# Loads of V issued on ScalarE's queue, loads of K on SyncE's

## The chip, the core and the metric

The kernel runs on one core of one Trainium2 chip. The core has five engines with instruction streams of their own (TensorE, VectorE, ScalarE, GpSimd, SyncE) and 16 DMA engines that move data from HBM to the on-chip memory SBUF. The metric is the device time of one execution in microseconds. Three executions of the kernel before took 669.8, 670.45 and 670.9 us; the median, 670.45 us, is the time that the change is measured against.

## The reference

One step of decoding with a cache, beside a gated MLP that shares its input. For 4 batch entries, 32 heads, 4096 cached positions and heads of 128 elements, all in bfloat16:

```python
xn = layernorm(x)                                   # x: (4, 1, 640)
q = (xn @ wq).reshape(B, Sq, H, Dh)                 # one query per head and batch entry
scores = einsum('bhqd,bhkd->bhqk', q, k_cache) * Dh ** -0.5
p = softmax(scores)
o = einsum('bhqk,bhkd->bhqd', p, v_cache)
out = x + o.reshape(B, Sq, H * Dh) @ wo + gmlp(xn)  # gmlp: w_in, gelu, layernorm, gate, w_out
```

K and V are read once each: 2 x 4 x 32 x 4096 x 128 elements of 2 bytes, 268 MB. The weights add some 14 MB. Each byte of the cache is used for one query alone, so the arithmetic is small beside the reading.

## The kernel before, in words

**Units.** The 32 heads are cut into `NG = 8` groups of `HG = 4`. A unit is one group and one batch entry, so there are `NU = 32` units, numbered u = 4g + b. Of each unit a K tile and a V tile of 4 MiB are loaded (128 partitions of 32 KiB): K0 to K31 and V0 to V31. Each is used in `NCH = 4` chunks.

**Buffers.** All these tiles, and before them three tiles of weights, come from one pool, `kvpool`, with five buffers that are handed out in turn. So the load of a tile waits until the tile five places earlier in the order of loads has been used up. The order alternates: K4, V0, K5, V1, K6, V2 and so on. So V(n) waits until K(n+2) is used up, and K(n) until V(n-7) is.

**What uses a tile.** A chunk of K is transposed by VectorE (`emit_T`, line 318, into `ktpool` with two buffers) and multiplied with the queries on TensorE (`emit_S`, line 336), which adds to the scores S of the group in PSUM. K is used up with its fourth transposition. When the scores of a group are complete, `softmax_max` and `softmax_exp` find the maximum and let ScalarE compute the exponentials (line 364), `softmax_t` transposes them on TensorE (line 377), and `z_fill` lets ScalarE copy them into the two operand buffers `Zb[0]` and `Zb[1]` (line 388; eight copies each). `emit_V` multiplies a chunk of V with them (line 422, eight matmuls); V is used up with its fourth chunk, 32 matmuls. After two units of V, `emit_O` copies the result from PSUM on ScalarE (line 430), and `emit_sel`, `emit_oT`, `emit_proj` bring it into the output projection.

**The order of the work.** One loop over steps s writes it down: K(u) is loaded at step 4u and transposed at 4u to 4u+3; V(v) is loaded at step 18 + 4v (`VD = 18`) and used at 18 + 4v to 21 + 4v; the softmax of group g stands at step 16g + 17. The framework (Tile) takes this as a priority, works out all waits, and may place an instruction ahead of another on its engine's stream where it reckons that it can start sooner.

**Queues.** All loads of K, V and wo stand on SyncE's queue, in the order of the source, each with its waits. ScalarE's queue issues three small loads at the start and half of the output at the end.

**The end.** V31 is treated apart: it is loaded in four pieces (`TAIL`, of 64, 32, 16 and 16 of its 128 rows), is the stationary operand of 128 small matmuls (line 534), and these wait for the pieces one by one. They accumulate in the one PSUM buffer (`ps_o`) that V30's result is copied out of first. After them come the projection (line 460) with `wo_last`, a cast and the output. `wo_last` is loaded in three pieces (line 299).

```python
        elif v == NU - 1 and vc == 0:
            g = NG - 1
            emit_O(g, 1)
            emit_selL(1, 1)
            ...
            ol_ps = ps_o.tile([P, HG], F32, tag="O", name="ol")
```

Of the kernel before, what the change touches and what calls it, by code (L numbers as in the profile page):

```python
# [16 lines left out]
def kernel(  # L17
# [19 lines left out]
    nc = tc.nc  # L37
    P = 128
    B, Sq, D = A_x.shape
    _, H, Sk, Dh = A_k_cache.shape  # L40
# [10 lines left out]
    NU = NG * B  # L51
# [33 lines left out]
    def kv_tile(name):  # L85
        return kvpool.tile([P, KV], BF16, tag="kv", name=name)
# [85 lines left out]
    for bb in range(2):  # L172
        nc.vector.tensor_copy(out=SelG[:, bb, :, :, 2 * bb:2 * bb + 2],
                              in_=I32[:].rearrange("p (b h c) -> p c h b", b=2, c=NCH))
# [13 lines left out]
    for hd in range(HG):  # L188
        nc.vector.tensor_copy(out=Pm[:, :, hd, :].rearrange("p (a w) j -> p a w j", w=2),
                              in_=ident_bf[:].rearrange("p (a j w) -> p a w j", a=2, w=2))  # L190
# [47 lines left out]
    t1 = const.tile([P, FC, B], F32)  # L238
# [45 lines left out]
    def load_unit(cache, key, u, cuts=(0, T)):  # L284
        g, b = divmod(u, B)
        t_sb = kv_tile(f"{key}{u}")
        src = cache[b, g * HG:(g + 1) * HG].rearrange("e (m t) d -> (e m) (t d)", t=T)
        for t0, t1 in zip(cuts[:-1], cuts[1:]):
            nc.sync.dma_start(out=t_sb[:, t0 * Dh:t1 * Dh], in_=src[:, t0 * Dh:t1 * Dh])
        state[(key, u)] = t_sb  # L290

    def load_wo(g):
# [197 lines left out]
    for s in range(NS):  # L490
        u, ch = divmod(s, NCH)
        if ch == 0 and u < NU:
            load_unit(A_k_cache, "k", u)
        v, vc = divmod(s - VD, NCH)
        if vc == 0 and 0 <= v < NU:
            load_unit(A_v_cache, "v", v, cuts=TAIL if v == NU - 1 else (0, T))
# [75 lines left out]
```

## Time and profile before

| What | Value |
|---|---|
| Median of three executions | 670.45 us |
| Profiled execution, its own time | 670.88 us |
| Its span, first to last instruction | 669.1 us |
| Moved by DMA in the span | 282.65 MB, 422 GB/s on the mean |
| Busy: TensorE / VectorE / ScalarE | 50% / 48% / 9% of the span |
| Loads of K and V, size and median time from issue to landing | 4 MiB; 43.3 us (K), 41.1 us (V) |
| Mean granted TensorE clock | 0.743 of full speed |

The span leaves out 1.8 us around the first and last instruction. A load's time from issue to landing holds the time that it waits behind earlier loads. In the profile, PE is TensorE, DVE is VectorE, ACT is ScalarE, SP is SyncE; a q behind the name (ACTq, SPq) is the engine's sequencer, which issues DMAs and handles waits.

### The profile page before, as it was taken

How to read it: one execution, taken by the hardware profiler on the slowest of the kernel's cores; microseconds unless marked ns; L12 is line 12 of the kernel's file. 1: busy time of each engine (PE TensorE's matmuls, PEld its weight loads, DVE VectorE, ACT ScalarE, POOL GpSimd, SP SyncE). 2: the span in 40 equal slices, each digit the busy share in tenths (PEclk: the TensorE clock that was granted, in tenths of full speed). 3: DMA queues.
4: the chain of work that ended last, by engine and by line, in shares of the span. 5: the costliest groups of instructions: out<-in, count | busy, mean ns of one | idle time of the engine just before them, and what ended most of it. 6: DMA issues, size and time to landing. Idle time of an engine off the chain costs nothing.

```text
span 669.1 us, 6401 instructions
## 1 busy us (share of the span) xinstructions
PE 335.7 (50%) x2781; PEld 139.1 (21%) x2781; DVE 319.5 (48%) x253; ACT 60.4 (9%) x184; POOL 8.9 (1%) x40
## 2 busy tenths in 40 slices
PE   0647463546543664337555364454753366433745
PEld 0511121122111221113121031111311122111323
DVE  4279853465533455542555534346543355543300
ACT  0200210012000210003000030001200021000300
POOL 0010000000000000000000000000000000000000
PEclk9997777778777787676766677866767878567676
DMA  8999999999999999999999999999999999999995
GB/s 313 439 424 428 436 433 428 425 436 431 426 435 430 428 434 439 424 428 434 427 429 433 432 427 434 426 427 441 428 431 430 431 427 432 433 433 426 435 418 230
DMA packets 12900, 282.65 MB, mean 422 GB/s; under 512 B 1621, under 2 KB 3017, under 8 KB 4169
## 3 DMA queue, kind: packets, MB, share of 16 engines
q1 hardware_dynamic: 12568, 282.25, 98.6%
q8 instruction: 21, 0.34, 0.2%
q10 hardware_dynamic: 304, 0.01, 0.0%
q14 instruction: 7, 0.05, 0.0%
HBM read 282.25 MB, written 0.01 MB: 422 GB/s over the span
## 4 chain that ended last, share of the span: by engine, by line
DMA 56%; PE 15%; issue 13%; DVE 12%; ACT 3%; ACTq 0%; DVEq 0%
DMA k<-in_A_k_cache_dram 50%; DVE kT L318 8%; PE O L422 6%; DMA wo_last<-in_A_wo_dram 5%; PE S L336 3%; ACT p L364 3%; PE misc L439 2%; DMA sb_bf<-in_B_b_sp_dram 2%; PE x L377 1%; DVE m L343 1%; DVE om L442 1%; PE misc L251 1%; PE misc L347 1%; ACT O_sb L430 0%; PE zT_ps L209 0%
## 5 line engine op out<-in xcount | busy, mean ns | idle before, releaser
L318 DVE STREAM_TRANSPOSE kT<-k 128x2048 f32<-128x2048 f32 x128 | 284.6, 2280 | 215.0 <-DMA k<-in_A_k_cache_dram 212.4
L336 PE MATMUL S<-kT,QZ 128*32 128x512 bf16 x1024 | 203.7, 538 | 257.6 <-DVE kT L318 255.2
L336 PEld LDWEIGHTS <-QZ 128*32 128x32 bf16 x1024 | 57.3, 115 | 399.1 <-issue 386.7
L422 PE MATMUL O<-v,Zb 128*32 128x512 bf16 x992 | 93.1, 467 | 9.0 <-DMA v<-in_A_v_cache_dram 9.0
L422 PEld LDWEIGHTS <-Zb 128*32 128x32 bf16 x992 | 42.1, 112 | 41.0 <-issue 26.2
L364 ACT ACTIVATE p<-S,negmax 128x1024 bf16<-128x1024 f32 x16 | 17.7, 1109 | 272.0 <-DVE negmax L358 272.0
L430 ACT COPY O_sb<-O 128x512 f32<-128x512 f32 x16 | 9.4, 585 | 240.6 <-PE O L422 240.6
L388 ACT COPY Zb<-x 32x128 bf16<-32x128 bf16 x128 | 27.3, 255 | 10.2 <-PE x L377 9.5
L377 PE MATMUL x<-IdP,p 128*128 128x128 bf16 x128 | 16.1, 305 | 18.9 <-ACT p L364 18.6
L442 DVE SCALAR_TENSOR_TENSOR om<-misc,rinv,MkH 16x512 bf16<-16x512 f32 x7 | 5.2, 739 | 37.8 <-PE misc L439 37.8
L439 PE MATMUL misc<-O_sb,SelG 128*16 128x128 f32 x112 | 16.9, 289 | 2.0 <-DVE rinv L398 1.5
L377 PEld LDWEIGHTS <-p 128*128 128x128 bf16 x128 | 12.0, 138 | 22.6 <-ACT p L364 22.6
L275 POOL COPY QZ<-q 32x16 bf16<-32x16 bf16 x32 | 7.9, 246 | 455.4 <-PE S L336 420.9
L439 PEld LDWEIGHTS misc<-O_sb,SelG 128*16 128x16 f32 x112 | 10.1, 99 | 7.9 <-ACT O_sb L430 2.4
L474 DVE TENSOR_TENSOR oL<-misc,rinv 128x8 bf16<-128x8 f32 (+1 forms) x2 | 0.3, 168 | 22.6 <-PE misc L472 22.6
L343 DVE TENSOR_REDUCE m<-S 128x1 f32<-128x512 f32 x8 | 5.5, 691 | 10.2 <-PE S L336 10.2
L147 PE MATMUL misc<-ident_bf,wq 4*128 4x4 bf16 x5 | 0.4, 178 | 18.9 <-DVE wq L143 18.9
L368 DVE TENSOR_TENSOR rowsum<-rs 128x1 f32<-128x1 f32 x8 | 1.2, 155 | 17.0 <-ACT p L364 17.0
L347 PE MATMUL misc<-dg,ones_f 128*128 128x128 f32 x16 | 3.9, 324 | 9.0 <-DVE dg L345 9.0
L364 ACT ACT_TABLE_LOAD x1 | 1.3, 1283 | 54.8 <-DVE negmax L358 54.8
L460 PE MATMUL proj<-wo,oT 128*4 128x320 bf16 x56 | 5.0, 298 | 1.9 <-DVE oT L453 1.9
L251 PE MATMUL misc<-xnT,wq 128*128 128x4 bf16 x160 | 4.7, 166 | 1.1 <-issue 0.8
(93 smaller groups left out, 75.9 us busy)
## 6 DMA issues: line engine op xcount, KB each, us to landing
k<-in_A_k_cache_dram SPq DMA_DIRECT2D x32, 4096.0 KB, 43.3
v<-in_A_v_cache_dram SPq DMA_DIRECT2D x31, 4096.0 KB, 41.1
wo<-in_A_wo_dram SPq DMA_DIRECT2D x7, 640.0 KB, 44.6
wq<-in_A_wq_dram SPq DMA_DIRECT2D x1, 3072.0 KB, 19.5
w_gmlp<-in_B_w_in_dram SPq DMA_DIRECT2D x1, 2160.0 KB, 9.3
wq<-in_A_wq_dram SPq DMA_DIRECT2D x1, 2048.0 KB
v<-in_A_v_cache_dram SPq DMA_DIRECT2D x1, 2048.0 KB
v<-in_A_v_cache_dram SPq DMA_DIRECT2D x1, 1024.0 KB, 38.4
```

The lines of the kernel that those rows point to most:

```text
L251: nc.tensor.matmul(q_ps[:, h, :], lhsT=wq_t[c][:, h * Dh:(h + 1) * Dh], rhs=xnT[:, c, :], start=(c == 0), stop=(c == DC - 1))
L318: nc.vector.transpose(kT[:], kw[:, ch * n:(ch + 1) * n])
L336: nc.tensor.matmul(S_ps[32 * q:32 * q + 32, :, :], lhsT=qz[:, b, kw, w0:w0 + 32], rhs=kT[:, i, :, kw // 2, :, kw % 2], start=(b == 0 and c ...
L343: nc.vector.tensor_reduce(out=m1[:], in_=S_ps[:].rearrange("p k m -> p (k m)"), axis=AX.X, op=ALU.max)
L347: nc.tensor.matmul(mm[:], lhsT=ones_f[:], rhs=dg[:], start=True, stop=True)
L364: nc.scalar.activation(out=p_i[:], in_=S_ps[:, 8 * i:8 * i + 8, None, :].to_broadcast((P, 8, HG, M)), func=ACT.Exp, bias=negmax[:, 0:1], s ...
L377: nc.tensor.transpose(x[:, t, :], p_bf[t // 8][:, t % 8].rearrange("p h m -> p (h m)"), IdP[:])
L388: nc.scalar.copy(out=dst, in_=src[:, 2 * bb + b1])
L422: nc.tensor.matmul(O_ps[32 * q:32 * q + 32, :, :], lhsT=Zb[bb][:, w0:w0 + 32], rhs=vv[:, e // 16, e % 16, :, :], start=(b1 == 0 and e < 4) ...
L430: nc.scalar.copy(out=O_sb[:], in_=O_ps[:])
L439: nc.tensor.matmul(oh[:], lhsT=SelG[:, bb, c].rearrange("p h b -> p (h b)"), rhs=O_sb[:, c, :], start=(bb == 0 and c == 0), stop=(bb == 1 ...
L442: nc.vector.scalar_tensor_tensor(out=om[:], in0=oh[:, None, :].to_broadcast((G, HG, Dh)), scalar=state.pop(("rinv", g))[:, 0:1], in1=MkH[: ...
```

## The change

The loads of V0 to V30 are issued by ScalarE, those of K and of V31, and of wo, still by SyncE. Sizes, buffers, waits for buffers and all other work are as they were.

```diff
     def load_unit(cache, key, u, cuts=(0, T)):
         g, b = divmod(u, B)
         t_sb = kv_tile(f"{key}{u}")
+
+        eng = nc.scalar if key == "v" and u < NU - 1 else nc.sync
         src = cache[b, g * HG:(g + 1) * HG].rearrange("e (m t) d -> (e m) (t d)", t=T)
         for t0, t1 in zip(cuts[:-1], cuts[1:]):
-            nc.sync.dma_start(out=t_sb[:, t0 * Dh:t1 * Dh], in_=src[:, t0 * Dh:t1 * Dh])
+            eng.dma_start(out=t_sb[:, t0 * Dh:t1 * Dh], in_=src[:, t0 * Dh:t1 * Dh])
         state[(key, u)] = t_sb
```

## The prediction

> **What bounds the kernel now.** I read the page's slices and queues first, then the waits of SyncE's queue, then the timeline of the last 30 us. The DMA row of the page (busy share of the DMA engines in 40 slices, and GB/s) and its list of queues:
>
> ```profile
> DMA  8999999999999999999999999999999999999995
> GB/s 313 439 424 428 436 433 428 425 436 431 426 435 430 428 434 439 424 428 434 427 429 433 432 427 434 426 427 441 428 431 430 431 427 432 433 433 426 435 418 230
> q1 hardware_dynamic: 12568, 282.25, 98.6%
> ```
>
> Only the first and the last slice are not full. Stretch by stretch the answer is the same; the last two columns are DMA share and GB/s:
>
> ```profile
> 500.00:600.00 100.00, 45.63 (x370) 18.21 (x368) 46.95 (x30) 7.38 (x23) 0.00 (x0) 0.75 1.00 430
> 660.00:665.00 5.00, 3.13 (x101) 2.80 (x99) 0.17 (x1) 0.00 (x0) 0.00 (x0) 0.52 0.42 154
> ```
>
> So the transfers bound the time, and one queue keeps them busy. SyncE's waits show why it does: loads wait for buffers (DVE: K used up; PE: V used up), long before their data are needed.
>
> ```profile
> SPq L289 <- DVE kT L318: 303.3, 32, 14.4
> SPq L289 <- DMA k<-in_A_k_cache_dram: 131.2, 30, 7.6
> SPq L289 <- PE O L422: 110.9, 27, 10.3
> ```
>
> At the end (TensorE's timeline from 644 us) the data come in the order of the queue, and TensorE waits for each:
>
> ```profile
> 644.46 3.60 PE L422 MATMUL O<-v,Zb 128*32 128x512 bf16 x32 [5.54 <-DMA v<-in_A_v_cache_dram]
> ...
> 654.18 3.19 PE L422 MATMUL O<-v,Zb 128*32 128x512 bf16 x32 [3.51 <-DMA v<-in_A_v_cache_dram]
> ...
> 658.06 1.06 PE L472 MATMUL misc<-I,O_sb 128*128 128x8 f32 x8 [0.47 <-ACT O_sb L430]
> 659.11 1.79 PE L534 MATMUL ol<-Zb,v 128*128 128x4 bf16 x64
> 661.58 1.02 PE L534 MATMUL ol<-Zb,v 128*128 128x4 bf16 x32 [0.68 <-DMA v<-in_A_v_cache_dram]
> ...
> 664.10 0.59 PE L534 MATMUL ol<-Zb,v 128*128 128x4 bf16 x16 [0.70 <-DMA v<-in_A_v_cache_dram]
> 664.95 1.28 PE L460 MATMUL proj<-wo_last,oL 128*4 128x320 bf16 x8 [0.26 <-DMA wo_last<-in_A_wo_dram]
> ```
>
> V29 lands at 644.4, V30 at 654.15, V31's last piece at 664.05: **9.75 us a load** at full rate. V30's work (654.18 to 659.11) is hidden under V31's transfer. After the last piece lie only 0.6 us of matmuls and the way out: 669.1 - 664.05 = 5.05 us.
>
> **What the Trainium skill says.**
> (1) "DMA: Bandwidth & Descriptors", Issuing engines are not separate DMA queues: transfers issued by different engines run on the same 16 DMA engines and interleave; a second issuer saves only issuing time. The trace agrees as far as it goes: 98.6% of 16 engines' span is already one queue's.
> (2) Same page, Queues, rings and completion order: each DMA engine goes round-robin between the rings that have work. I read that as half the rate for each of two busy rings. No run here shows it: ScalarE's queue is idle through the loop.
> (3) Same page, Where 436 GB/s comes from: the ports' ceiling is 435.2 GB/s. The trace's 430 to 431 is 1% below.
> (4) "Perfetto Trace Analysis", DMA Instruction — HWDGE: the issuing sequencer itself waits for a DMA's semaphores before it goes on. So whatever stands behind a waiting load on ScalarE's stream waits too, and a load behind a waiting instruction of the sequencer is late. The trace has such waits on ScalarE: one before nearly each copy of O, for V's matmuls.
>
> ```profile
> L430 ACTq EVENT_SEMAPHORE  x14: 17/17/17, 155.3 to 648.1; - x14
> ```
>
> **The change part by part.**
>
> *Issue.* 31 issues of 0.33 us (SyncE's timeline: 0.33 for each load of V) leave SyncE and come to ScalarE: 10.2 us over a span in which ScalarE is busy 60.4 us. Cost 0, hidden under the transfers; without that cover at most one issue before each of 8 exponentials, 2.6 us. SyncE gains nothing: it waits for buffers, not for itself.
>
> *Place in ScalarE's stream.* Decisive. Is V(n)'s load placed where the source has it (step 18+4n, when V(n) is needed at once), or where its buffer comes free (K(n+2) used up, step 4n+11)? The trace shows that streams are not in source order. The source has eight copies of Zb, the copy of O, eight copies of Zb; ScalarE's timeline has nine, one, seven:
>
> ```profile
> 230.21 1.97 ACT L388 COPY Zb<-x 32x128 bf16<-32x128 bf16 x9 [1.13 <-PE x L377]
> 234.26 0.58 ACT L430 COPY O_sb<-O 128x512 f32<-128x512 f32 x1 [2.08 <-PE O L422]
> 234.74 1.54 ACT L388 COPY Zb<-x 32x128 bf16<-32x128 bf16 x7
> ```
>
> TensorE too runs four chunks of S and then 32 matmuls of V, where the source alternates. So instructions go where they are reckoned ready, and I take it that V's loads keep about their present times. Then ScalarE's work stands well to them: V(4g+1) waits for K(4g+3), which the exponentials need anyway. At worst the exponentials of group g stand behind V(4g+2), which waits for K(4g+4).
>
> *Middle of the kernel.* With two rings at half rate, K(n+4) and V(n) land together, 19.5 us after the pair before, instead of K first and V 9.75 later. Let a pair land at t. K's four transpositions (8.9 us: 254.72 to 263.61 in VectorE's timeline) free its buffer at t+8.9. V's matmuls free the other by t+12, or, at a group's end, by about t+20 (before: K31's transpositions start at 613.84, V27's matmuls end at 633.3). The pair landing at t+19.5 was issued before t. The pair after needs its loads at t+19.5: V's comes at t+8.9, K's by t+20 at the worst, so one ring at least always has work. In the worst order (exponentials behind V(4g+2)): K(4g+4) is used up at t+28.4, V(4g) at t+28.4+8+3 = t+39.5; K(4g+7) is issued then, and its turn is at t+58.5. The transfers never run dry: cost 0. What two interleaved streams do to the rate itself, no row shows. Bounds: up to the ceiling, 1% or 6.3 us gained over 656 us of transfers; 2%, 13 us, lost, the spread of the page's slices about 430. I take 0.
>
> *End.* K30 and V26 land at 604 (V26's matmuls start at 604.12 now; the bytes moved by then are the same), K31 and V27 at 623.4; K31 now lands at 613.8, so it is a load later. From 623.4 ScalarE's ring holds V28, V29, V30; SyncE's is empty until K31 is used up, 623.4+8.9 = 632.3, when V31's pieces are issued (now 622.75). V28 runs alone, to 633. Then V29 and V31 share: both land near 652.5. **V30 is last**, alone, whole. Group 7's exponentials (now 12.4 us, Zb 17.6 us after K31's landing, so about 641) are in time. All bytes are moved when they are now, except that the first two pieces of wo_last (0.48 MB, 1.1 us), now behind V31, come before V30's end: V30 lands at 664.05 + 1.1 = 665.2. After it: 4.93 us to the first matmul on V31 (654.18 to 659.11: matmuls, copy, selection; `ol` needs V30's PSUM buffer, so it can't go ahead), 128 matmuls at 1.79/64 = 3.6 us, and 4.4 us to the end (664.69 to 669.1). Sum 12.9 after landing, where now 5.05 follow. The third piece of wo_last is issued at 654.15 now, at V30's landing; it has these 8.5 us to come, hidden.
>
> Sum: 1.1 + 12.9 - 5.05 = **+9.0 us**. Against the profiled execution: span 678.1, its time 679.9; it stands 0.4 above the median, so **679.4 us**, between 675 and 685.
>
> **The rivals.**
> *Source order on ScalarE (13%).* If loads stand at their source place, V(4g) and V(4g+1) are issued only after the exponentials of g, V(4g+2) and V(4g+3) only after the copy of O of the first two. Each half group is a chain: first V at half rate 19.5, second alone to 29, its use 9 to 12, copy 0.6: 41 us; the other half adds the softmax, 8 us (S's end 623.85 to Zb 631.7): 49. A group takes 90, now 80.9 (exponentials 226.79 to 307.65): 7 x 9 = +64, **735 us**. For it: those sequencer waits, and x_res, ready since its memset at 11.9 us, whose load stays behind waiting loads until 606.5. Against it: nine, one, seven.
> *The interleaving costs rate (10%)*: up to 3% beside the end's loss, 685 to 705 us, say **693**. Against it: large rows from either stream.
> *V31 still lands last (8%)*: decided from V31's issue on: at 632.3 ScalarE's ring has some 19.5 us of data, SyncE's 11; V31 must come about 9 us later, or ScalarE's ring be favoured. Then the end is as now, **670.5 us**.
> *Faster (5%): the rate.* Two rings at the ceiling give -6.3, which does not outweigh +9.0 by itself; the other side is reached from a gain of 10.3 us, 437.9 GB/s. That is over the ceiling of (3), though single slices show 439 and 441. Say 440: **665 us**.
>
> **How the numbers follow.** Likeliest 64%: 679.4 (675 to 685). The range 670 to 705 takes in V31-last and the rate's loss and leaves out source order and faster, 18%. A measurement of this kernel tells 0.2%, 1.3 us, from no change. Faster is the rate case, 0.05; same is V31-last, 0.08; slower the rest, 0.87.
>
> **What would show it.** Right: DMA share 1.00 at 430 in the middle; K and V landing in pairs; issue to landing shorter for V than for K at first; DMA again idle only from about 663; V30's 32 matmuls the last to wait for a transfer, then 128 matmuls in one run without waits. Wrong: DMA share under 0.95 in the middle, with TensorE waiting for V of each first or third unit of a group (source order); pieces of V31 still awaited at the end; GB/s off 430.

## The result, and the profile after

| | Before | After |
|---|---|---|
| Median of four executions each | 670.33 us (669.8 to 670.9) | 690.88 us (689.14 to 691.64) |
| Span of the profiled execution | 669.1 us | 689.8 us |
| Mean granted TensorE clock | 0.743 | 0.704 |
| Loads of K / V, median from issue to landing | 43.3 / 41.1 us | 36.5 / 26.3 us |

The ratio is 1.0303, with a 95% interval of 1.028 to 1.0326: the changed kernel is some 20.5 us slower. The forecast was slower by 9.0, so it had the sign and less than half the size. In spans, which the traces can take apart, 678.1 us were forecast and 689.8 measured. Where these 11.7 us came from is the question of this part.

The page of the changed kernel, its slices and its queues (each slice is now 17.2 us; q1 is SyncE's queue, q10 ScalarE's, followed by packets, MB and share of the DMA engines' time):

```profile
DMA  8999999999999999999999999999999999992991
GB/s 314 435 431 433 425 429 437 433 426 433 431 428 432 429 427 430 432 436 430 428 431 428 429 435 424 433 435 430 428 427 431 432 430 433 431 406 105 439 439 44
q1 hardware_dynamic: 8104, 152.23, 51.9%
q10 hardware_dynamic: 4768, 130.03, 43.9%
```

Up to slice 35 nothing has changed: the DMA engines are full at the old rate, now from two queues. Then two things differ from before. One slice near the end, the 37th (621 to 638 us), falls to 105 GB/s; and the last slice, with 44 GB/s, holds nearly no transfers, where before it had 230. The stretches of the changed kernel show the first of them closely (columns: bounds, length, busy PE, PEld, DVE, ACT and POOL, granted clock, DMA share, GB/s):

```profile
500.00:600.00 100.00, 50.91 (x424) 19.50 (x421) 48.43 (x31) 7.21 (x23) 0.00 (x0) 0.73 1.01 431
620.00:640.00 20.00, 8.70 (x66) 3.56 (x69) 10.90 (x11) 2.30 (x4) 0.00 (x0) 0.67 0.36 142
624.00:626.00 2.00, 0.00 (x0) 0.00 (x0) 2.00 (x1) 0.00 (x0) 0.00 (x0) 0.50 0.00 0
626.00:633.00 7.00, 4.91 (x34) 1.73 (x35) 6.83 (x4) 0.00 (x0) 0.00 (x0) 0.74 0.00 0
```

Before, the stretch from 620 to 640 had a share of 1.00 at 427 GB/s. Now it moves 142: 20 x (1 - 142/430) = **13.4 us of transfers are missing**, and from 624 to 633 nothing moves at all. That no load was possible then is not the reason. ScalarE's timeline shows when the loads of V27 to V30 were issued (the four lines with ACTq), and between what:

```profile
599.50 0.58 ACT L432 COPY O_sb<-O 128x512 f32<-128x512 f32 x1 [25.00 <-PE S L338]
599.52 0.34 ACTq L291 DMA_DIRECT2D v<-in_A_v_cache_dram  x1
636.42 1.11 ACT L366 ACTIVATE p<-S,negmax 128x1024 bf16<-128x1024 f32 x1 [36.34 <-DVE negmax L360]
636.53 0.34 ACTq L291 DMA_DIRECT2D v<-in_A_v_cache_dram  x1
...
644.70 0.68 ACT L390 COPY Zb<-x 32x128 bf16<-32x128 bf16 x3
645.21 0.33 ACTq L291 DMA_DIRECT2D v<-in_A_v_cache_dram  x1
645.28 0.52 ACT L390 COPY Zb<-x 32x128 bf16<-32x128 bf16 x2
645.59 0.45 ACTq L291 DMA_DIRECT2D v<-in_A_v_cache_dram  x1
```

V28's buffer is V25's. It was free at 599.5, when ScalarE copied the result of V24 and V25. V29's is K30's, whose last transposition ended at 603.5, and V30's is V26's, whose last matmul ended at 629.05. They were issued at 636.53, 645.21 and 645.59: 37, 42 and 17 us late. In the stream V28 stands behind the first exponential of group 7, and that waits 36.34 us for the maximum, which needs K31. V29 and V30 stand among the copies of `Zb`.

The end, in TensorE's timeline:

```profile
664.90 3.60 PE L424 MATMUL O<-v,Zb 128*32 128x512 bf16 x32 [6.70 <-DMA v<-in_A_v_cache_dram]
669.24 1.88 PE L474 MATMUL misc<-I,O_sb 128*128 128x8 f32 x8 [0.74 <-ACT O_sb L432]
675.87 3.61 PE L424 MATMUL O<-v,Zb 128*32 128x512 bf16 x32 [4.76 <-DMA v<-in_A_v_cache_dram]
680.17 1.87 PE L474 MATMUL misc<-I,O_sb 128*128 128x8 f32 x8 [0.69 <-ACT O_sb L432]
681.89 3.55 PE L536 MATMUL ol<-Zb,v 128*128 128x4 bf16 x128
685.71 1.23 PE L462 MATMUL proj<-wo_last,oL 128*4 128x320 bf16 x8 [0.26 <-DVE oL L537]
```

V30's 32 matmuls are the last that wait for a transfer, and the 128 matmuls on V31 follow in one run without a wait, as forecast. V30 landed at 675.87, and 13.9 us follow; before, V31's last piece landed at 664.05, and 5.05 followed. The landing is 11.8 later and the work behind it 8.9 us longer: together the 20.7 us between the spans.

### The profile page after: what moved, and what is told of

Its sections match the earlier page's. It is cut to its first block, busy times and chain, and to the rows that moved or that the text cites. A ratio compares the mean times of both kernels' runs of the same rounds, so it can differ in the third digit from the quotient of the medians.

```text
span 689.8 us, 6412 instructions
## 1 busy us (share of the span) xinstructions
PE 320.8 (47%) x2781; PEld 129.7 (19%) x2781; DVE 319.6 (46%) x253; ACT 59.8 (9%) x184; POOL 9.0 (1%) x40
## 4 chain that ended last, share of the span: by engine, by line
DMA 73%; PE 9%; DVE 9%; issue 7%; ACT 1%; ACTq 0%; DVEq 0%
DMA k<-in_A_k_cache_dram 52%; DMA v<-in_A_v_cache_dram 20%; DVE kT L320 6%; PE O L424 4%; PE S L338 2%; DMA sb_bf<-in_B_b_sp_dram 1%; PE x L379 1%; PE misc L251 1%; PE ol L536 0%; PE zT_ps L209 0%; DVE m L345 0%; PE proj L267 0%; ACT Zb L390 0%; PE misc L474 0%; DVE om L444 0%
## 5 line engine op out<-in xcount | busy, mean ns | idle before, releaser
L338 PE MATMUL S<-kT,QZ 128*32 128x512 bf16 x1024 | 190.1, 511 | 212.8 <-DVE kT L320 202.6
L424 PE MATMUL O<-v,Zb 128*32 128x512 bf16 x992 | 118.8, 559 | 110.7 <-DMA v<-in_A_v_cache_dram 110.7
L424 PEld LDWEIGHTS <-Zb 128*32 128x32 bf16 x992 | 38.7, 123 | 168.2 <-issue 124.8
L366 ACT ACTIVATE p<-S,negmax 128x1024 bf16<-128x1024 f32 x16 | 17.7, 1109 | 228.3 <-DVE negmax L360 228.3
L441 PE MATMUL misc<-O_sb,SelG 128*16 128x128 f32 x112 | 13.8, 273 | 1.1 <-DVE rinv L400 0.7
L379 PE MATMUL x<-IdP,p 128*128 128x128 bf16 x128 | 11.0, 244 | 6.3 <-ACT p L366 6.3
L379 PEld LDWEIGHTS <-p 128*128 128x128 bf16 x128 | 8.6, 109 | 12.5 <-ACT p L366 6.9
L462 PE MATMUL proj<-wo,oT 128*4 128x320 bf16 x56 | 7.4, 382 | 0.3 <-DVE oT L455 0.3
## 6 DMA issues: line engine op xcount, KB each, us to landing
k<-in_A_k_cache_dram SPq DMA_DIRECT2D x32, 4096.0 KB, 36.5
v<-in_A_v_cache_dram ACTq DMA_DIRECT2D x31, 4096.0 KB, 26.3
```

Source lines behind the costliest of these rows:

```text
L338: nc.tensor.matmul(S_ps[32 * q:32 * q + 32, :, :], lhsT=qz[:, b, kw, w0:w0 + 32], rhs=kT[:, i, :, kw // 2, :, kw % 2], start=(b == 0 and c ...
L366: nc.scalar.activation(out=p_i[:], in_=S_ps[:, 8 * i:8 * i + 8, None, :].to_broadcast((P, 8, HG, M)), func=ACT.Exp, bias=negmax[:, 0:1], s ...
L379: nc.tensor.transpose(x[:, t, :], p_bf[t // 8][:, t % 8].rearrange("p h m -> p (h m)"), IdP[:])
L424: nc.tensor.matmul(O_ps[32 * q:32 * q + 32, :, :], lhsT=Zb[bb][:, w0:w0 + 32], rhs=vv[:, e // 16, e % 16, :, :], start=(b1 == 0 and e < 4) ...
L441: nc.tensor.matmul(oh[:], lhsT=SelG[:, bb, c].rearrange("p h b -> p (h b)"), rhs=O_sb[:, c, :], start=(bb == 0 and c == 0), stop=(bb == 1 ...
L462: nc.tensor.matmul(proj[32 * hf:32 * hf + B, 0:NO2], lhsT=oT[:, c, :], rhs=wo_t[:, c, hf * NO2:(hf + 1) * NO2], start=False, stop=(last an ...
```

## The experiments

The theory at this point: the 13.4 us are lost because V28 to V30 stand in ScalarE's stream behind group 7's softmax, when no load of K is left to cover them; the rest is the exposed end of V30, landing last and whole; the middle costs nothing. Its rivals: two rings at work cost something by themselves; K31 and with it the softmax of group 7 come late (K31's first transposition is at 623.95, before at 613.84) and everything behind them; or the order of landing alone explains it all. A fourth is the granted clock, 0.704 on the mean where it was 0.743. The first four runs shared one chip and a kernel before at 670.25 us.

**The last four loads of V on SyncE.** V28 to V30 go back to SyncE's queue, where V31's pieces are already. V0 to V27 stay on ScalarE's queue, so two rings work through nine tenths of the kernel:

```diff
-        eng = nc.scalar if key == "v" and u < NU - 1 else nc.sync
+        eng = nc.scalar if key == "v" and u < NU - 4 else nc.sync
```

> V28 to V30 go back to SyncE's queue, V0 to V27 stay on ScalarE's. Theory (the loss lies at the end alone: V28 to V30 are issued behind group 7's exponentials, so the transfers run dry for 13 us, and V30 lands last and whole, 7.3 us): both are gone, 670.5 us, ratio 0.998 to 1.004, no dry stretch in the DMA row. Rival 1 (two rings cost in themselves, all through the loop): still 685 to 691. Rival 2 (K31 lands a load later, at 624 where it was 613.8, and the softmax of group 7 with it sets the end): 675 to 681.

Measured: 670.51 us, ratio 1.0005 (0.9996 to 1.0014). The page of this run, its stretch from 620 us, ScalarE's first exponential of group 7 and TensorE's last wait for V31:

```profile
DMA  8999999999999999999999999999999999999996
620.00:640.00 20.00, 9.82 (x75) 3.80 (x75) 10.90 (x11) 2.30 (x4) 0.00 (x0) 0.67 0.99 424
635.01 1.11 ACT L366 ACTIVATE p<-S,negmax 128x1024 bf16<-128x1024 f32 x1 [36.24 <-DVE negmax L360]
663.33 0.59 PE L536 MATMUL ol<-Zb,v 128*128 128x4 bf16 x16 [0.66 <-DMA v<-in_A_v_cache_dram]
```

The stretch is full again, and V31's last piece lands last, at 663.33. The first exponential of group 7 still starts late, at 635.01. So neither two rings nor the late K31 cost anything here: the whole 20.5 us hang on the loads of V28 to V30. Nor does a lower clock by itself: executions of this kernel at 0.718 and at 0.745 took 670.12 and 670.28 us.

**V28 to V30 on ScalarE, but ahead of its softmax.** Nothing changes queue; the three loads are written right behind V27's:

```diff
-        if vc == 0 and 0 <= v < NU:
+        if vc == 0 and (0 <= v < NU - 4 or v == NU - 1):
             load_unit(A_v_cache, "v", v, cuts=TAIL if v == NU - 1 else (0, T))
+        if s == NCH * (NU - 1) + 2:
+            for w in range(NU - 4, NU - 1):
+                load_unit(A_v_cache, "v", w)
```

> V28 to V30 stay on ScalarE's queue, but are written right after V27, so that they stand ahead of group 7's exponentials; V31 stays on SyncE's. Theory: the dry 13 us are gone, V30 still lands last and whole: the prediction's own sum, 678 to 680 us, ratio 1.011 to 1.015. Rival 1: 688 to 691, as with the change. Rival 2: 675 to 681, so this run alone doesn't tell it from the theory.

Measured: 676.2 us, ratio 1.0088 (1.0073 to 1.0103). ScalarE's timeline, the stretch, and the end on TensorE:

```profile
598.16 31.53 ACTq L291 DMA_DIRECT2D v<-in_A_v_cache_dram  x4
636.63 1.11 ACT L366 ACTIVATE p<-S,negmax 128x1024 bf16<-128x1024 f32 x1 [37.91 <-DVE negmax L360]
```

```profile
620.00:640.00 20.00, 10.14 (x92) 4.22 (x91) 10.96 (x12) 3.13 (x7) 0.00 (x0) 0.72 1.00 429
```

```profile
660.79 3.60 PE L424 MATMUL O<-v,Zb 128*32 128x512 bf16 x32 [7.59 <-DMA v<-in_A_v_cache_dram]
665.09 1.87 PE L474 MATMUL misc<-I,O_sb 128*128 128x8 f32 x8 [0.69 <-ACT O_sb L432]
666.81 3.55 PE L539 MATMUL ol<-Zb,v 128*128 128x4 bf16 x128
```

With the same queue, the dry stretch is gone: the place in the stream made it. The measured time is below the theory's 678 to 680 and in the range of the rival that blamed K31; the run before speaks against that rival, since K31 was as late there. The miss is in the end, 5.7 us of span instead of some 9. V30 lands at 660.79, and 14.0 us follow, so the work behind it has its full length; but V30 comes earlier than V31's last piece did before. From 655 to 662 us SyncE's queue (V31's pieces and `wo_last`) still moves 1.9 MB, 0.60 MB of it after V30's landing: the two rings run out nearly together.

**All of V on ScalarE, early.** As the run before, and V31's four pieces too go to ScalarE's queue, behind V30:

```diff
-        eng = nc.scalar if key == "v" and u < NU - 1 else nc.sync
+        eng = nc.scalar if key == "v" else nc.sync
...
-            for w in range(NU - 4, NU - 1):
-                load_unit(A_v_cache, "v", w)
+            for w in range(NU - 4, NU):
+                load_unit(A_v_cache, "v", w, cuts=TAIL if w == NU - 1 else (0, T))
```

> As the run before, and V31's four pieces too are issued on ScalarE's queue behind V30, ahead of group 7's exponentials: all of V on one ring, all of K on the other. Theory: no dry stretch, and V31's pieces land last again: 670.5 us, ratio 0.998 to 1.005. Rival 1: 685 to 691. Rival 2: 675 or more.

Measured: 672.34 us, ratio 1.0034 (1.0021 to 1.0047), so 2.1 us slower than before. The stretch, ScalarE's issues with the exponential behind them, and TensorE's last wait:

```profile
620.00:640.00 20.00, 8.73 (x74) 3.02 (x73) 10.50 (x9) 0.00 (x0) 0.00 (x0) 0.76 0.99 428
599.16 44.79 ACTq L291 DMA_DIRECT2D v<-in_A_v_cache_dram  x8
644.05 1.11 ACT L366 ACTIVATE p<-S,negmax 128x1024 bf16<-128x1024 f32 x1 [44.33 <-DMA v<-in_A_v_cache_dram]
665.35 0.59 PE L539 MATMUL ol<-Zb,v 128*128 128x4 bf16 x16 [0.67 <-DMA v<-in_A_v_cache_dram]
```

V31's pieces land last again, and the exposed end is gone. The eight issues hold ScalarE's stream so long that the exponentials of group 7 start only at 644.05; V28 and V29 then run under the transfers of V30 and V31. The last piece is awaited at 665.35, where before it was 664.05. Why it comes 1.3 us later stays open. With V31 gone from SyncE, `wo_last` is issued there at 636.06 and moves beside V31's pieces; but that its 0.64 MB now go ahead is not the reason, for in the kernel before, too, all but 0.04 MB had moved when V31's last piece landed.

**V31 ahead of V30, on one queue.** The kernel before, with the last two loads swapped; no second queue at all:

```diff
-        if vc == 0 and 0 <= v < NU:
-            load_unit(A_v_cache, "v", v, cuts=TAIL if v == NU - 1 else (0, T))
+        if vc == 0 and 0 <= v < NU - 2:
+            load_unit(A_v_cache, "v", v)
+        elif vc == 0 and v == NU - 2:
+            load_unit(A_v_cache, "v", NU - 1, cuts=TAIL)
+            load_unit(A_v_cache, "v", NU - 2)
```

> The kernel before with its one queue; only the loads of V31's pieces are issued ahead of V30's, so that V30 lands last and whole. Theory: the exposed end by itself, 7 to 9 us: 677.5 to 679.5, ratio 1.010 to 1.014, with no transfer dry. If the order of landing is not what the end costs: 670.5.

Measured: 678.9 us, ratio 1.0126 (1.0109 to 1.0143), +8.6. TensorE's timeline:

```profile
663.63 3.61 PE L422 MATMUL O<-v,Zb 128*32 128x512 bf16 x32 [13.47 <-DMA v<-in_A_v_cache_dram]
667.17 0.43 PE L311 MATMUL proj<-x_res,ident_bf 32*4 32x320 bf16 x2
667.92 1.87 PE L472 MATMUL misc<-I,O_sb 128*128 128x8 f32 x8 [0.33 <-ACT O_sb L430]
669.65 3.55 PE L537 MATMUL ol<-Zb,v 128*128 128x4 bf16 x128
```

The bytes come as early as before; only their order differs. This is the end that the prediction priced at 9.0, by itself.

**V28 alone back on SyncE** (a kernel before at 670.49 us beside it):

```diff
-        eng = nc.scalar if key == "v" and u < NU - 1 else nc.sync
+        eng = nc.scalar if key == "v" and u < NU - 1 and u != NU - 4 else nc.sync
```

> The changed kernel, but the load of V28 alone is issued on SyncE's queue again, behind K31; V29 and V30 stay behind ScalarE's exponentials of group 7, and V30 still lands last. If the dry stretch is caused by where V28 to V30 stand in ScalarE's stream (theory): V28 fills the stretch from about 619 to 629 us, the transfers are dry only from there to V31's pieces (about 632.9) and again from about 642.6 until V29 is issued at 645.2, together about 6.5 us in place of about 13, and the exposed end of V30 stays at about 7: about 684 us, ratio 1.019 to 1.023. If the lost 13 us come from two rings or from the end's order and not from late issue (rivals): about 690 us, ratio 1.03. If the whole loss hung on V28 alone: about 677 us, ratio 1.01.

Measured: 679.39 us, ratio 1.0136 (1.0119 to 1.0153). This lies below what the theory said and above what "all on V28" said. Its stretch and ScalarE's timeline:

```profile
620.00:640.00 20.00, 10.99 (x82) 4.61 (x81) 10.90 (x11) 2.30 (x4) 0.00 (x0) 0.67 0.93 391
```

```profile
634.26 1.11 ACT L366 ACTIVATE p<-S,negmax 128x1024 bf16<-128x1024 f32 x1 [35.39 <-DVE negmax L360]
634.45 0.34 ACTq L291 DMA_DIRECT2D v<-in_A_v_cache_dram  x1
...
643.04 0.33 ACTq L291 DMA_DIRECT2D v<-in_A_v_cache_dram  x1
```

Only 20 x (1 - 391/430) = 1.8 us are missing, where 6.5 were expected. The expectation kept V29 at 645.2, but V29 has moved into the place behind the first exponential that V28 left, and was issued at 634.45; and V28, issued at 598.2 and sharing with others, landed about 35.6 us later, near 633.8 rather than 629. V30 landed at 662.76, and 14.1 us follow: the exposed end is as in the changed kernel. Late issue of V28, with the place that it takes from V29, made nearly all of the dry stretch. Why the framework leaves one load at that place and the next among the copies of `Zb` stays open.

**All of V on ScalarE, at its late places** (a kernel before at 670.37 us beside it). The same line as in the third run, and no load moved: the dry stretch without the exposed end.

```diff
-        eng = nc.scalar if key == "v" and u < NU - 1 else nc.sync
+        eng = nc.scalar if key == "v" else nc.sync
```

> The changed kernel with V31's four pieces on ScalarE's queue too, behind V30, all at their places in the source. V28 to V30 stay as late as in the changed kernel, but V31 lands last again, so this shows the dry stretch without the exposed end of V30. By the theory: transfers run dry from about 623 us until V28 is issued at about 636.5, and V31's pieces no longer fill the last 3.5 us of it: about 16 us lost in place of 13.4; then full to the end, V31's last piece 1.5 us later for the pieces of wo_last ahead of it, and the old end of about 5 us behind it: span about 686.5, time 688, ratio 1.025 to 1.028. If the late issue cost nothing and the order of the end were the whole loss: about 672, as in the run with all of V on ScalarE issued early. Before V31's pieces lies the copy of O on ScalarE, which waits for V29; if that comes after V30 has landed, a second dry stretch adds to it.

Measured: 688.07 us, ratio 1.0253 (1.0232 to 1.0274), and a span of 686.3. Stretches, and the end on TensorE:

```profile
620.00:640.00 20.00, 9.92 (x66) 3.79 (x69) 10.91 (x11) 2.30 (x4) 0.00 (x0) 0.59 0.20 74
640.00:675.00 35.00, 18.92 (x164) 8.65 (x156) 1.34 (x4) 4.76 (x19) 0.00 (x0) 0.65 0.99 422
```

```profile
677.00 3.25 PE L536 MATMUL ol<-Zb,v 128*128 128x4 bf16 x112
681.32 0.59 PE L536 MATMUL ol<-Zb,v 128*128 128x4 bf16 x16 [1.07 <-DMA v<-in_A_v_cache_dram]
```

20 x (1 - 74/430) = 16.6 us are missing, V31's last piece lands at 681.3, and 5.0 follow, as before the change. So the dry stretch costs its full length at the end, by itself.

| Kernel | Dry stretch | V30 last | Against before, us |
|---|---|---|---|
| last four on SyncE | no | no | +0.3 |
| all V on ScalarE, early | no | no | +2.1 |
| V28 to V30 early | no | yes, V31 beside it | +5.9 |
| one queue, V31 ahead | no | yes | +8.6 |
| V28 alone on SyncE | 1.8 | yes | +8.9 |
| all V on ScalarE, late | 16.6 | no | +17.7 |
| the change | 13.4 | yes | +20.5 |

By itself the dry stretch of 16.6 us cost 17.7, and the exposed end 8.6; with neither, 0.3 and 2.1 us were lost. The two causes as they stand in the changed kernel, 13.4 and 8.6, add to 22.0 against the 20.5 measured, so they explain it within 1.5 us. None of these kernels beats the one before.

## Why the prediction was right in sign and wrong in size

*Issue* (0): right. ScalarE's issues took 0.33 to 0.45 us each, and the run with 28 of the 31 loads on ScalarE was level with before.

*Middle of the kernel* (0, and the rate unchanged): right. From 500 to 600 us the share is 1.01 at 431 GB/s. It is right although loads of V were late there too: V20 was issued at 475.14, just behind an exponential that started at 474.95, and V21 and V22 behind copies of `Zb` at 483.06 and 486.12, while the transfers went on (SyncE's ring held loads of K meanwhile):

```profile
474.95 1.11 ACT L366 ACTIVATE p<-S,negmax 128x1024 bf16<-128x1024 f32 x1 [35.05 <-DVE negmax L360]
475.14 0.34 ACTq L291 DMA_DIRECT2D v<-in_A_v_cache_dram  x1
460.00:500.00 40.00, 16.55 (x149) 7.11 (x149) 24.68 (x18) 6.11 (x21) 0.98 (x4) 0.71 1.00 430
```

TensorE waited for V, and it cost nothing; its waits for V grew from 9.0 us to

```profile
PE O L424 <- DMA v<-in_A_v_cache_dram: 110.7, 18, 11.7
```

(us, times, longest). A long wait of an engine that is not the bound says little.

*Place in ScalarE's stream*: **this step failed.** It was called decisive, and decided by one sign, that copies of `Zb` had been moved over the copy of O. From this it took that loads of V are put where their buffers come free, and keep "about their present times". They don't: V28 was 37 us late, and the transfers ran dry for 13.4 us. Group 7 was not alone in this: counted in the order of issue, V12, V20 and V28 stand just behind the first exponential of their groups 3, 5 and 7, while V8, V16 and V24 stand ahead of those of groups 2, 4 and 6; only behind V28 was no load of K left. The bad case that the step did name was the reverse one, exponentials standing behind a load. A load standing behind exponentials was only thought of in the rival of source order.

*End*: its base failed with that step. "From 623.4 ScalarE's ring holds V28, V29, V30" was wrong: it held none until 636.5. That V30 would land last and whole was right, and so was the sign, for the reason given. The arithmetic of the end was near. V30 was to land at 665.2 and landed at 675.87, 10.7 later: 13.4 us dry, less 2.7, since without these it would have landed at 662.5. (The three runs with V30 last and little or nothing dry show 660.8, 662.8 and 663.6.) Of these 2.7 us, 1.1 are the term for the pieces of `wo_last`, which was wrong: before, too, all but 0.04 MB had moved when the last piece of V31 landed. The other 1.6 stay open. Behind it were to come 12.9 us, and 13.9 came: from V30's first matmul to the first on V31 it took 6.02 us instead of 4.93, chiefly as the selection took 1.87 instead of 1.06. The work was the same and the granted clock was not: 0.50 in this stretch, 0.73 on the mean before. In the run with the last four loads on SyncE, at a clock of 1.00, V30's matmuls took 1.91 us instead of 3.61 and the selection 1.06. Together -2.7 + 1.0 + 13.4 = 11.7, the whole miss. The half rate that was taken for each of two rings does not hold in this end either, as the last section shows.

*The rivals.* Source order had the mechanism half right, loads of V behind exponentials and behind copies, and its price wrong: it let each half group pay (+64), where K's ring covers all but the last. It said nothing of that last one by itself, which is what happened. The loss of rate, V31 landing last and the gain of rate did not occur. That the wide range, 670 to 705 us, holds the measured time is luck: its upper part was there for the loss of rate, and it was a dry stretch that filled it.

The Trainium skill's sentences agree with the traces as far as they go. Engines that issue don't add DMA bandwidth ("DMA: Bandwidth & Descriptors", Issuing engines are not separate DMA queues): 430 GB/s from one queue, 430 to 431 from two. And the sequencer that issues a DMA itself waits for its semaphores before it goes on ("Perfetto Trace Analysis", DMA Instruction — HWDGE). The page says this of a DMA; here it was the wait of an exponential that held up the load behind it, whose buffer was free at 599.5 and which was issued at 636.53. The prediction named both cases when it cited the page, and worked out only what a waiting load holds up.

## What to carry to other kernels

A queue is fed by an instruction stream: before loads are moved to another engine, read in that engine's timeline what it waits for, longest first, and assume that a load can stand behind each of these waits unless the compiled order shows otherwise. Late loads are free while another ring still holds work, so look at the stretch where that ring runs out, as a rule near the end: here a dry stretch there cost its full length, 17.7 us for 16.6. And two queues give up a fixed order of landing: the load to end last should be the one with the least work behind it, here 5 us against 13 to 14.

## What had not been expected of the hardware

Two rings with work share packet for packet, and not byte for byte, where the prediction took half the rate for each. With V28 alone back on SyncE, both rings held whole tiles from 600 to 621 us, 32 KB to a partition, and moved 4.55 and 4.53 MB in 155 and 156 packets. With V28 to V30 early, ScalarE's ring held whole tiles from 635 to 655 us and SyncE's the pieces of V31, of 16 KB to a partition and less. The packets were again about as many, the bytes were not (packets, MB, share of the DMA engines):

```profile
q10 hardware_dynamic: 202, 5.90, 68.7%
q1 hardware_dynamic: 209, 2.62, 30.8%
```

In the changed kernel it was 7.27 MB in 238 packets against 1.28 MB in 231, from 640 to 660 us. So here the ring with the large pieces got most of the bytes, and V30 was ahead of V31's small ones. In the run with V28 to V30 early, V30 landed at 660.79 with 0.60 MB still to move on SyncE's ring, where with one queue it landed at 663.63, behind all of V31; the exposed end cost 5.9 us instead of 8.6.
